# One transfer of 128 rows per tile for the last stores of an attention and SwiGLU kernel, in place of two of 64 rows

## The chip, the cores and the metric

The kernel runs on one core of a Trainium2 chip. The metric is the device time of one execution in microseconds (us); the figure quoted for a kernel is the median of its runs. One further execution is taken with the hardware profiler. Its "span" runs from the first to the last instruction on the core, and its own device time is a little longer than that span.

## The reference

```python
def _attn_ref(q, k, v):                       # each (8, 8, 576, 64), float32
    ...
    def phi(x, c, s):
        r = np.maximum(x, 0.0)
        return np.concatenate([r * c, r * s], axis=-1)
    q_p = phi(q, cos_w, sin_w)
    k_p = phi(k, cos_w, sin_w)
    kv = np.einsum('bhsf,bhsd->bhfd', k_p, v)
    z = np.sum(k_p, axis=2)
    num = np.einsum('bhsf,bhfd->bhsd', q_p, kv)
    den = np.einsum('bhsf,bhf->bhs', q_p, z)[..., None] + 1e-06
    return (num / den).astype(np.float32)

def _moe_ref(x, w_gate, w_val, w_out):        # x (4608, 512); weights 512x1536, 512x1536, 1536x512
    g = x @ w_gate
    silu = g * (1.0 / (1.0 + np.exp(-g)))
    val = x @ w_val
    return (silu * val @ w_out).astype(np.float32)

def reference(**kwargs):
    attn_out = _attn_ref(...)
    x = np.ascontiguousarray(attn_out.transpose(0, 2, 1, 3)).reshape(B * S, H * D)
    return _moe_ref(x=x, ...)
```

The output is 4608 rows of 512 float32 values, 9.44 MB.

## The kernel before

The linear attention of the eight batches is computed first for each batch, and its 4608 rows then go through the gated feed-forward block in nine groups (`tg` 0 to 8) of 512 rows. In each group the gate and value projections (line 990) are followed by the output product (line 1155); from group 1 on these products are done on 2x2 blocks, with seven block products in place of eight, so that sums of blocks stand beside them (`P1` to `P7` in `out_jobs`). Attention of later batches runs beside the feed-forward work of earlier groups.

Nothing is scheduled at run time. Every piece of work is a `Job` with a function, an engine and the jobs after which it comes; a table of job numbers, `ORDER`, says in which order the jobs are written into the program. Each engine then runs its own instructions in that order. The planner's figures in a `Job` (engine costs, `tail`, `dma`) aren't used when the table is there, except for the names of the engines.

An output tile is 128 rows of a group; a group has four (`t0` to `t0 + 3`). Rows of one batch are numbered so that a partition holds every ninth row:

```python
    out_v = out.rearrange("(b p c) f -> b c p f", p=SH, c=NC)      # SH = 64, NC = 9
```

So `out_v[b, c]` is 64 rows of the output that lie 9 x 512 values apart, and a tile of 128 partitions is two such sets: partitions 0 to 63 hold `c`, partitions 64 to 127 hold `c + 1`. The address in memory goes from row to row of one set by 4608 values, and from one set to the next by 512.

The results wait in SBUF in `ob` (groups 0 to 7) or, for the last group, in a part of `r_q` (`ob_last`), and are stored from there:

- `store_jobs` (line 1118) stores a tile of 512 columns by two transfers of 64 rows. In group 7, the second-last, tiles `t0` and `t0 + 1` go through the queue of SyncE (SP) and tiles `t0 + 2` and `t0 + 3` through that of GpSimd (POOL). The groups before use POOL alone, but for the first.
- In the last group each result quarter (256 columns of two tiles) is stored as it gets ready. `store_two_jobs` (line 1248) stores 64 rows of two tiles in one transfer, `store_tile_jobs` (line 1257) stores 64 rows of one tile. Of each pair one goes through SP's queue and the other through that of ScalarE (ACT).

The quarters of the last group get ready in this order: `e11` (tiles `t0`, `t0 + 1`, columns 0 to 255, one ACT operation, line 632), `e22` (tiles `t0 + 2`, `t0 + 3`, columns 256 to 511, two DVE operations, line 1212), `e21` (the same tiles, columns 0 to 255, two DVE operations, line 636) and `e12` (tiles `t0`, `t0 + 1`, columns 256 to 511, two DVE operations, line 636).

Transfers that SP and ACT issue signal their end through eight semaphores (`DMAHW0` to `DMAHW7`) that are taken in turn. A transfer waits, before it is issued, until the one eight places before it on these two queues has landed.

Of the kernel before, what the change touches and what calls it, by code (L numbers as in the profile page):

```python
# [18 lines left out]
def kernel(  # L19
# [10 lines left out]
    nc = tc.nc  # L30
# [4 lines left out]
    SH = 64  # L35
    NC = S // SH
    d_model, d_ff = moe_w_gate.shape
# [7 lines left out]
    NTG = NH // GH  # L45
# [4 lines left out]
    HD = d_model // 2  # L50
# [132 lines left out]
    def idle_products(n, cols=P):  # L183
# [34 lines left out]
        out=tab.rearrange("p c e d -> p (c e) d"),  # L218
        in_=csk.rearrange("p c e -> p (c e)").to_broadcast([P, NC * 2, D]),
# [31 lines left out]
    for j in range(2):  # L251
        t = (phi_all.rearrange("p a b -> p (a b)")[:, 0:V2_1].rearrange(
            "p (g c e w) -> p g c e w", g=G, c=NC, e=2) if j else
            consts.tile([P, G, NC, 2, W], BF16, name=f"v2_{j}"))
# [259 lines left out]
    for word in words:  # L514
        word, _, eng = word.partition("@")
        op, a, b = re.match(r"([A-Za-z]+)(\d+)\.?(\d*)", word).groups()
# [95 lines left out]
    def copies(n):  # L612
        return {"ACT": sc(n)}
# [24 lines left out]
    def relu_on(eng, out, in_):  # L638
        relu_op("act" if eng == "ACT" else "dve", out, in_)
# [25 lines left out]
    out_v = out.rearrange("(b p c) f -> b c p f", p=SH, c=NC)  # L665
# [450 lines left out]
        return res  # L1116

    def store_jobs(t, after, put, queues, cols=slice(0, d_model)):
        for e in range(2):
            q_ = queues[e]  # L1120

            def fn(j, e=e):
                idx = 2 * t + e
                {"POOL": nc.gpsimd, "SP": nc.sync, "ACT": nc.scalar}[j.eng].dma_start(  # L1124
                    out=out_v[idx // NC, idx % NC][:, cols], in_=ob_of(t)[e * SH:(e + 1) * SH, cols])
            Job({q_: 535 if q_ == "POOL" else 610}, fn, after=after, put=put, tail=1500.0, dma=(1450.0, 480.0))

    obs = {}

    def ob_of(t):  # L1130
        return pair_of(t // 2)[:, t % 2]

    def pair_of(p):
        return (ob_last if obs[p].kind == "last ob" else ob_all)[:, obs[p].at[0]]

    def out_jobs(tg, key):
        last = tg == NTG - 1
        t0 = tg * OUT
        ts = token_sum_jobs(tg)
        rooms = {n: Room("last ob" if last else "ob") for n in range(2)}  # L1140
# [6 lines left out]
        def product(n, rs, a, b, first, after, get=(), parts=((range(HC), (0, 1)),), keys=()):  # L1147

            res = []
            for m, (kcs, its) in enumerate(parts):  # L1150
                def fn(j, kcs=kcs, its=its):
                    for kc in kcs:
                        for i in its:
                            to = ps(rs[0])[:, i] if len(rs) == 1 else bank(rs[i])[:, 0:HD]
                            nc.tensor.matmul(out=to, lhsT=a[:, kc, i * P:(i + 1) * P], rhs=b[:, kc],  # L1155
                                             start=first and kc == 0 and i == 0, stop=kc == HC - 1, skip_group_check=True)
                at = keys[m] if m < len(keys) else (key[0], key[1] + (n + m / 4) * key[2])
                res.append(pe(len(kcs) * len(its) * 109.15, fn, at, after=after(kcs, its), behind=res, get=get if not m else ()))
            return res
# [3 lines left out]
        a, e = Room("bank", fills=True), Room("bank", fills=True)  # L1163
# [3 lines left out]
        def blk(w, jh):  # L1167
            return lambda kcs, its: blocks_of(tg, w, jh, sorted({kc // 2 for kc in kcs}))

        def summed(n, *more):  # L1170
            return lambda kcs, its: [ts[n][h] for h in sorted({kc // 4 for kc in kcs})] + tsum + sum(more, [])
# [31 lines left out]
            copied(j.eng, C(0, 0), ps(a), DOWN)  # L1203
        e11 = Job(copies(512), fn, after=P2, get=[rooms[0]], put=[a])
        if last:
            store_two_jobs(t0, slice(0, HD), [e11], ("SP", "ACT"))
        P5 = product(4, bs, S1, T1, False, lambda kcs, its: summed(1)(kcs, its) + ([ads[its[0]]] if last else ads), (), two)
        e22 = []
        for n, b_ in enumerate(bs):
# [2 lines left out]
                nc.vector.scalar_tensor_tensor(out=x, in0=p_, scalar=DOWN, in1=x, op0=ALU.mult, op1=ALU.add)  # L1212
            e22.append(Job({"DVE": d1(256 if last else 512)}, fn, after=P5[n:n + 1], behind=e22[-1:]))
        if last:
            store_two_jobs(t0 + 2, slice(HD, d_model), e22, ("SP", "ACT"))
        P4 = product(5, cs, aq[:, 1, 1], T4, False, lambda kcs, its: ([ads[its[0]]] if last else ads) + tsum + blk(1, 1)(kcs, its), (), two)
        e21 = []
        for n, c in enumerate(cs):
# [2 lines left out]
            e21.append(Job({"DVE": d1(256)} if last else copies(512), fn, after=P4[n:n + 1], put=[c]))  # L1221
        if last:
            for n in range(2):
                store_tile_jobs(t0 + 2, n, slice(0, HD), [e21[n]])
        else:
            for t in (t0 + 2, t0 + 3):
                store_jobs(t, e22 + e21, [rooms[1]], ("POOL", "POOL"))
        P3 = product(6, bs, S4, bq[:, 1, 1], False, lambda kcs, its: ts[4] + ([e22[its[0]]] if last else e22), (), two,
                     () if last or tg not in P3_AT else [(tg + 1, P3_AT[tg])])
        e12 = []  # L1230
# [4 lines left out]
            e12.append(Job({"DVE": d1(256)} if last else copies(512), fn, after=P3[n:n + 1], put=[b_]))  # L1235
        if last:
            for n in range(2):
                store_tile_jobs(t0, n, slice(HD, d_model), [e12[n]])
        else:
            for t in (t0, t0 + 1):  # L1240
                store_jobs(t, [e11] + e12, [rooms[0]], ("SP", "SP") if tg == NTG - 2 else ("POOL", "POOL"))
        J_["products", tg] = dict(P1=P1, P2=P2, P3=P3, P4=P4, P5=P5, P6=P6, P7=P7)
        J_["ht_free", tg, 0, 0] = P1 + ts[3] + ts[2]
        J_["ht_free", tg, 0, 1] = P5 + ts[2]
        J_["ht_free", tg, 1, 0] = P2 + ts[4]
        J_["ht_free", tg, 1, 1] = P4 + ts[1]

    def store_two_jobs(t, cols, after, queues):
        for e in range(2):
            def fn(j, e=e):  # L1250
                (b, c), (b1, _) = divmod(2 * t + e, NC), divmod(2 * t + 2 + e, NC)
                assert b == b1
                {"SP": nc.sync, "ACT": nc.scalar}[j.eng].dma_start(
                    out=out_v[b, c:c + 3:2, :, cols].rearrange("c p f -> p c f"),
                    in_=pair_of(t // 2)[e * SH:(e + 1) * SH, :, cols])
            Job({queues[e]: 660}, fn, after=after, tail=1300.0, dma=(700.0, 560.0))

    def store_tile_jobs(t, i, cols, after, queues=("SP", "ACT")):
        for e in range(2):
            def fn(j, e=e):  # L1260
                b, c = divmod(2 * (t + i) + e, NC)
                {"SP": nc.sync, "ACT": nc.scalar}[j.eng].dma_start(
                    out=out_v[b, c][:, cols], in_=pair_of(t // 2)[e * SH:(e + 1) * SH, i, cols])
            Job({queues[e]: 620}, fn, after=after, tail=1300.0, dma=(700.0, 280.0))

    def plain_out_jobs(key):
        rooms = [Room("ob"), Room("ob")]
# [33 lines left out]
    for lo, hi in ((0, 2), (2, 4)):  # L1301
        def fn(j, lo=lo, hi=hi):
            o = raws[1, "k"][:, lo:hi]
            relu_on(j.eng, o, o)
# [118 lines left out]
    for tg in range(1, NTG):  # L1423
        b = tg + 2
# [20 lines left out]
        for u in range(3):  # L1445
# [9 lines left out]
            rooms, silus = silu_jobs(tg, u, block_jobs(tg, u, "G", gate_order(tg, u)))  # L1455
# [3 lines left out]
            else:  # L1459
                for n, (i, w) in enumerate(((0, 0), (0, 1), (1, 0), (1, 1))):  # L1460
                    plain_val(tg, u, i, w, rooms, silus, at[f"v{n}"])
        out_jobs(tg, (tg, 3.05, 0.9 / 7))


# [69 lines left out]
    """  # L1534

    todo = set(jobs)
    for word in ORDER.split():
        n, e, at = re.match(r"(\d+)([av]?):?([\d,]*)", word).groups()
        j, at = jobs[int(n)], [int(x) for x in (at.split(",") if "," in at else at)]
# [36 lines left out]
```

## Time and profile before

| what | value |
|---|---|
| time, median of 3 runs | 299.13 us (298.21 to 299.59) |
| the profiled execution's own time | 298.66 us |
| its span | 296.8 us (so 1.86 us lie outside it) |
| TensorE (PE) busy | 290.1 us, 98% of the span |
| VectorE (DVE) / ScalarE (ACT) / GpSimd (POOL) busy | 252.9 / 199.1 / 69.1 us |
| mean granted TensorE clock | 0.996 |
| the last copy into the output buffer (DVE, line 636) | starts at 291.89 us, takes 0.42 us |
| stores of SP and ACT in the profile's end part | 10 on SP, 6 on ACT |

A profile line of instructions gives start, duration, engine, line of the kernel, operation and tiles written and read. "SPq" and "ACTq" are the issuing of transfers by these engines. The DMA rows give, for a stretch of time, the busy share of the 16 DMA engines and the rate in 40 equal slices (a digit is a tenth), then packets, MB and the time of these packets as a share of 16 engines for each queue. Queue q1 is SP's, q10 is ACT's and q0 POOL's. One packet here is one row of a store; small packets of 4 bytes come on top of them.

### The profile page before, as it was taken

Reading aid. Unit: us, or ns where it says so; the run is one execution under the profiler, and the core shown is the slowest. Engines: PE = TensorE matmul, PEld = TensorE weight load, DVE = VectorE, ACT = ScalarE, POOL = GpSimd, SP = SyncE. Lnnn points to the kernel's source line nnn. Section 1 sums busy time; section 2 is a strip of 40 time slices with the busy share of each in tenths; the row PEclk is TensorE's granted clock in tenths of the full one; section 3 lists DMA queues with packets and bytes.
Section 4 is the critical chain, followed back from the end, with each engine's and each line's share of the span. In section 5 each row is a group of like instructions: output and inputs, shape, how many; then the busy total and the mean of one; then the engine's idle time right before and its main releaser. Section 6 shows DMA issues by size and latency. Waiting matters only on the chain.

```text
span 296.8 us, 8157 instructions
## 1 busy us (share of the span) xinstructions
PE 290.1 (98%) x3292; PEld 237.7 (80%) x3292; DVE 252.9 (85%) x513; ACT 199.1 (67%) x423; POOL 69.1 (23%) x122
## 2 busy tenths in 40 slices
PE   8999999999999999999999999999999999999993
PEld 4697455665877888988898898888988898888882
DVE  7976889889987899999898977998778968968882
ACT  6664347978479868985499689976566555564630
POOL 7963530012015012213343020400050032002000
PEclk9999999999999999999999999999999999999998
DMA  7999999999969999599959947980270036000226
GB/s 255 232 196 198 202 206 209 229 202 155 170 149 171 199 209 144 102 172 148 209 118 159 197 68 131 208 146 2 38 171 8 2 89 127 0 2 18 55 53 161
DMA packets 71973, 40.90 MB, mean 138 GB/s; under 512 B 48768, under 2 KB 68736, under 8 KB 71936
## 3 DMA queue, kind: packets, MB, share of 16 engines
q0 software_dynamic: 24800, 24.39, 49.9%
q1 hardware_dynamic: 46528, 15.47, 27.6%
q10 hardware_dynamic: 608, 0.52, 0.6%
q8 instruction: 26, 0.43, 0.6%
q14 instruction: 11, 0.09, 0.1%
HBM read 37.75 MB, written 9.44 MB: 159 GB/s over the span
## 4 chain that ended last, share of the span: by engine, by line
PE 87%; DMA 9%; DVE 2%; issue 0%; DVEq 0%
PE banks L990 43%; PE banks L1155 23%; DMA xT<-x 4%; DMA phit<-r_q 4%; PE banks L440 4%; PE banks L917 4%; PE banks L1275 3%; PE banks L789 3%; PE banks L718 2%; PE banks L1065 2%; DMA wo_sb<-in_v_dram 1%; DVE v L292 1%; PE banks L371 1%; PE banks L784 1%; PE banks L1323 0%; PE banks L314 0%
## 5 line engine op out<-in xcount | busy, mean ns | idle before, releaser
L1124 POOL DMA_DIRECT2D out_dram<-ob x52 | 27.3, 532 | 128.4 <-ACT ob L632 87.6
L630 ACT COPY banks<-banks 128x512 f32<-128x512 f32 (+1 forms) x53 | 30.4, 577 | 22.3 <-PE banks L990 9.9
L1049 ACT ACTIVATE sg<-banks 128x512 bf16<-128x512 f32 x72 | 40.9, 599 | 5.8 <-PE banks L990 5.6
L1085 DVE TENSOR_TENSOR ht<-sg,banks 128x512 f16<-128x512 bf16 x60 | 40.4, 682 | 4.8 <-PE banks L990 4.4
L1155 PEld LDWEIGHTS <-ht 128*128 128x128 f16 x384 | 37.5, 98 | 4.5
L990 PEld LDWEIGHTS <-wg_sb 128*128 128x128 f16 x384 | 36.7, 98 | 5.3
L990 PEld LDWEIGHTS <-wgs_sb 128*128 128x128 f16 x368 | 35.4, 98 | 6.4 <-issue 0.5
L1010 DVE TENSOR_TENSOR banks<-m,banks 128x512 f32<-128x512 f32 x44 | 30.2, 692 | 7.3 <-PE banks L990 6.0
L990 PEld LDWEIGHTS <-wv_sb 128*128 128x128 f16 x320 | 31.2, 98 | 3.7
L990 PE MATMUL banks<-kvt,wgs_sb 128*128 128x256 f16 x236 | 33.8, 273 | 0.3 <-DVE kvt L963 0.3
L1155 PEld LDWEIGHTS <-sums 128*128 128x128 f16 x288 | 28.0, 98 | 3.4
L630 ACT COPY m<-banks 128x512 f32<-128x512 f32 x44 | 25.5, 590 | 5.7 <-PE banks L990 5.7
L990 PE MATMUL banks<-xT,wg_sb 128*128 128x256 f16 x192 | 28.6, 273 | 0.0
L632 ACT ACTIVATE ob<-banks 128x512 f32<-128x512 f32 x32 | 19.1, 596 | 10.6 <-PE banks L1155 9.3
L1155 PE MATMUL banks<-wo_sb,ht 128*128 128x256 f16 x192 | 25.2, 273 | 0.0
L990 PE MATMUL banks<-kvt,wg_sb 128*128 128x256 f16 x168 | 24.4, 273 | 0.0
L1155 PE MATMUL banks<-wt_sb,sums 128*128 128x256 f16 x192 | 24.2, 273 | 0.0
L820 DVE TENSOR_TENSOR x<-banks,rec 128x512 f16<-128x512 f32 x31 | 21.3, 690 | 3.1 <-PE banks L990 0.5
L990 PE MATMUL banks<-xT,wv_sb 128*128 128x256 f16 x160 | 23.8, 273 | 0.0
L1155 PE MATMUL banks<-wt_sb,ht 128*128 128x256 f16 x192 | 22.8, 272 | 0.0
L890 ACT ACTIVATE r_q<-raw_q,tanq 128x256 bf16<-128x256 bf16 x45 | 20.1, 507 | 0.0
L292 DVE TENSOR_TENSOR v<-raw_kv,tab 128x1152 bf16<-128x1152 bf16 x27 | 19.9, 750 | 0.0
(160 smaller groups left out, 540.1 us busy)
## 6 DMA issues: line engine op xcount, KB each, us to landing
out_dram<-ob POOLq DMA_DIRECT2D x52, 128.0 KB, 3.3
raw_kv<-in_k_dram POOLq DMA_DIRECT2D x7, 576.0 KB, 6.2
raw_q<-in_q_dram POOLq DMA_DIRECT2D x12, 288.0 KB, 9.9
raw_kv<-in_v_dram POOLq DMA_DIRECT2D x6, 576.0 KB, 9.3
out_dram<-ob SPq DMA_DIRECT2D x12, 128.0 KB, 2.8
wg_sb<-in_moe_w_gate_dram POOLq DMA_DIRECT2D x5, 256.0 KB, 9.0
wv_sb<-in_moe_w_val_dram POOLq DMA_DIRECT2D x5, 256.0 KB, 9.6
wo_sb<-in_v_dram SPq DMA_DIRECT2D x2, 576.0 KB, 4.1
```

Source lines behind the costliest of these rows:

```text
L292: nc.vector.tensor_tensor(out=v2s[b == 1][:, g, :, :, 0:D], in0=(first if b == 0 and g == 0 else {"v": raw_of(b, "v")})["v"][:, g].unsquee ...
L440: nc.tensor.matmul(out=st["f", tg, fc, lo][i], lhsT=(wg_sb, wv_sb)[i][:, kc, fs], rhs=xT[tg][:, ts, kc], start=(kc == 0), stop=(kc == KC - 1))
L630: nc.scalar.copy(out=out, in_=in_)
L632: nc.scalar.mul(out=out, in_=in_, mul=mul)
L820: tt(out=x_.rearrange("p (i y d) -> p i y d" if pairs else "p (y e d) -> p e y d", d=D, **({"i": 2} if pairs else {"e": 2})), in0=view()[: ...
L890: nc.scalar.activation(out=home()[:, :, c, 1], in_=raws[b, "q"][:, :, c], func=AF.Relu, scale=tanq[:, c:c + 1])
L990: nc.tensor.matmul(out=to[:, i], lhsT=a[:, c, 2 * u + i], rhs=x()[:, :, c], start=first and i == 0 and c == 0, stop=c == KH - 1, skip_grou ...
L1010: tt(out=bank(c), in0=one(m7_all, m).rearrange("p i x -> p (i x)"), in1=bank(b), op=ALU.add)
L1049: nc.scalar.activation(out=gates(rooms[w])[:, :, jh * HT:(jh + 1) * HT], in_=src, func=AF.Silu, scale=DOWN)
L1085: tt(out=ht[:, 4 * u + w:4 * u + w + 3:2, jh * HT:(jh + 1) * HT], in0=gates(rooms[w])[:, :, jh * HT:(jh + 1) * HT], in1=src.rearrange("p ( ...
L1124: {"POOL": nc.gpsimd, "SP": nc.sync, "ACT": nc.scalar}[j.eng].dma_start(out=out_v[idx // NC, idx % NC][:, cols], in_=ob_of(t)[e * SH:(e + ...
L1155: nc.tensor.matmul(out=to, lhsT=a[:, kc, i * P:(i + 1) * P], rhs=b[:, kc], start=first and kc == 0 and i == 0, stop=kc == HC - 1, skip_gro ...
```

## The change

Every store of the last group now carries one tile of 128 rows and 256 columns, and SP's stores of the second-last group carry one tile of 128 rows and 512 columns. The memory side of such a transfer is `out_v[b, c:c + 2]`, a view of 2 x 64 rows; the SBUF side is 128 partitions. POOL's stores and those of group 0 stay as they are. In `e22`'s stores, each waits for its own tile instead of for both.

```diff
     def store_jobs(t, after, put, queues, cols=slice(0, d_model)):
+        if len(queues) == 1 and 2 * t % NC < NC - 1:
+            return whole_tile_job(t, cols, after, queues[0], put, 6500.0)
         for e in range(2):
-            q_ = queues[e]
+            q_ = queues[e % len(queues)]
...
+    def whole_tile_job(t, cols, after, queue, put=(), tail=1300.0):
+
+        def fn(j):
+            b, c = divmod(2 * t, NC)
+            {"POOL": nc.gpsimd, "SP": nc.sync, "ACT": nc.scalar}[j.eng].dma_start(
+                out=out_v[b, c:c + 2][:, :, cols], in_=ob_of(t)[:, cols])
+        Job({queue: 600}, fn, after=after, put=list(put), tail=tail, dma=(700.0, 560.0))
...
         if last:
-            store_two_jobs(t0, slice(0, HD), [e11], ("SP", "ACT"))
+            for n in range(2):
+                whole_tile_job(t0 + n, slice(0, HD), [e11], ("SP", "ACT")[n])
...
         if last:
-            store_two_jobs(t0 + 2, slice(HD, d_model), e22, ("SP", "ACT"))
+            for n in range(2):
+                whole_tile_job(t0 + 2 + n, slice(HD, d_model), e22[n:n + 1], ("SP", "ACT")[n])
...
             for n in range(2):
-                store_tile_jobs(t0 + 2, n, slice(0, HD), [e21[n]])
+                whole_tile_job(t0 + 2 + n, slice(0, HD), [e21[n]], ("SP", "ACT")[n])
...
             for n in range(2):
-                store_tile_jobs(t0, n, slice(HD, d_model), [e12[n]])
+                whole_tile_job(t0 + n, slice(HD, d_model), [e12[n]], ("SP", "ACT")[n])
...
-                store_jobs(t, [e11] + e12, [rooms[0]], ("SP", "SP") if tg == NTG - 2 else ("POOL", "POOL"))
+                store_jobs(t, [e11] + e12, [rooms[0]], ("SP",) if tg == NTG - 2 else ("POOL", "POOL"))
...
-        1418:6 1406 1411 1412 1413 1409 1420 1426 1422 1423 1427 1308 1421:1 1428:0 1310 1309 1312 1429 1311 1410 1414
+        1416:6 1404 1409 1410 1411 1407 1418 1424 1420 1421 1425 1308 1310 1309 1419:1 1426:0 1428 1427 1408 1412
```

The rest of `ORDER` is the same jobs under numbers that are lower by two. On TensorE, VectorE and GpSimd the instructions and their order are the same as before.

On SyncE's queue the program ended with these stores (the size is that of the memory side, `ob` and `r_q` are the SBUF tiles, and the brackets name what is waited for):

```order
L1124 DMA out_dram<-ob 64x512 [waits DMAHW0_49,Activation_49]
L1124 DMA out_dram<-ob 64x512 [waits DMAHW1_49]
L1124 DMA out_dram<-ob 64x512 [waits DMAHW2_49]
L1253 DMA out_dram<-r_q 64x2x256 [waits DMAHW4_49,Activation_49]
L1124 DMA out_dram<-ob 64x512 [waits DMAHW5_49]
L1253 DMA out_dram<-r_q 64x2x256 [waits DMAHW7_49,DVE_49]
L1262 DMA out_dram<-r_q 64x256 [waits DMAHW1_49,DVE_49]
L1262 DMA out_dram<-r_q 64x256 [waits DMAHW3_49,DVE_49]
L1262 DMA out_dram<-r_q 64x256 [waits DMAHW5_49,DVE_49]
L1262 DMA out_dram<-r_q 64x256 [waits DMAHW7_49,DVE_49]
```

Ten transfers stand there, and each has 64 as the first of its memory side's dimensions. At the same place, from the last transpose on, SyncE now has these:

```order
L749 DMA_TRANSPOSE xT<-x 128x4x128 [waits DMAHW7_49,DVE_49]
L1134 DMA out_dram<-ob 2x64x512 [waits DMAHW0_49,Activation_49]
L1134 DMA out_dram<-ob 2x64x512 [waits DMAHW1_49]
L1134 DMA out_dram<-r_q 2x64x256 [waits DMAHW3_49,Activation_49]
L1134 DMA out_dram<-r_q 2x64x256 [waits DMAHW4_49,DVE_49]
L1134 DMA out_dram<-r_q 2x64x256 [waits DMAHW6_49,DVE_49]
L1134 DMA out_dram<-r_q 2x64x256 [waits DMAHW0_49,DVE_49]
```

Six transfers take the place of ten, the two of `ob` stand next to each other ahead of those of `r_q`, the first dimension on the memory side is 2, and the last one waits on the semaphore of the first store of `ob`.

On ScalarE's queue the six stores before were these:

```order
L1253 DMA out_dram<-r_q 64x2x256 [waits DMAHW3_49,Activation_49]
L1253 DMA out_dram<-r_q 64x2x256 [waits DMAHW6_49,DVE_49]
L1262 DMA out_dram<-r_q 64x256 [waits DMAHW0_49,DVE_49]
L1262 DMA out_dram<-r_q 64x256 [waits DMAHW2_49,DVE_49]
L1262 DMA out_dram<-r_q 64x256 [waits DMAHW4_49,DVE_49]
L1262 DMA out_dram<-r_q 64x256 [waits DMAHW6_49,DVE_49]
```

They come behind the last ACT operation, that of `e11`. From that operation on, ScalarE now has these:

```order
L632 ACTIVATE r_q<-banks 128x2x256 [waits PE_49]
L1134 DMA out_dram<-r_q 2x64x256 [waits DMAHW2_49,Activation_49]
L1134 DMA out_dram<-r_q 2x64x256 [waits DMAHW5_49,DVE_49]
L1134 DMA out_dram<-r_q 2x64x256 [waits DMAHW7_49,DVE_49]
L1134 DMA out_dram<-r_q 2x64x256 [waits DMAHW1_49,DVE_49]
```

Four transfers take the place of six, and the last of them waits on the semaphore of SP's second store of `ob`.

More of the change, by code (lines that the diff above doesn't have):

```diff
@@ L1125, in fn @@
                     out=out_v[idx // NC, idx % NC][:, cols], in_=ob_of(t)[e * SH:(e + 1) * SH, cols])
-            Job({q_: 535 if q_ == "POOL" else 610}, fn, after=after, put=put, tail=1500.0, dma=(1450.0, 480.0))
+            Job({q_: 560}, fn, after=after, put=put, tail=6500.0, dma=(1270.0, 480.0))
+    def whole_tile_job(t, cols, after, queue, put=(), tail=1300.0):
[4 more added lines that the diff above has]
+        Job({queue: 600}, fn, after=after, put=list(put), tail=tail, dma=(700.0, 560.0))
     obs = {}
@@ L1246, in out_jobs @@
         J_["ht_free", tg, 1, 1] = P4 + ts[1]
[L1248 to L1264, printed above, removed]
     def plain_out_jobs(key):
```

21 rows, old and new, of the table ORDER are left out of this document.

## The prediction

> **What bounds the kernel now.** I read the page first, for the engine that limits the span, then the chain of waits, and then the end of the trace: the queues of SyncE (SP) and ScalarE (ACT), and the DMA view in short stretches.
>
> ```profile
> span 296.8 us, 8157 instructions
> PE 290.1 (98%) x3292; PEld 237.7 (80%) x3292; DVE 252.9 (85%) x513; ACT 199.1 (67%) x423; POOL 69.1 (23%) x122
> ...
> 282.68 9.18 PE banks L1155 x84
> 291.87 0.02 issue
> 291.89 0.42 DVE r_q L636
> ```
>
> TensorE is busy for 98% of the span and the chain runs through it to 291.87 us. One DVE copy follows and ends at 291.89 + 0.42 = 292.31. The change leaves all instructions of TensorE, VectorE and GpSimd in place, so nothing before the first changed store, at 285.20, can move. What the change can touch is what lies behind 292.31: 296.8 - 292.31 = 4.5 us in which only stores are issued, moved and waited for. The SP and ACT queues there, from the timeline:
>
> ```profile
> 285.20 1.76 SPq L1124 DMA_DIRECT2D out_dram<-ob  x3
> 288.58 0.65 SPq L1253 DMA_DIRECT2D out_dram<-r_q  x1
> 289.28 0.61 SPq L1124 DMA_DIRECT2D out_dram<-ob  x1
> 289.99 1.16 SPq L1253 DMA_DIRECT2D out_dram<-r_q  x1
> ...
> 288.59 2.56 ACTq L1253 DMA_DIRECT2D out_dram<-r_q  x2
> 291.25 2.82 ACTq L1262 DMA_DIRECT2D out_dram<-r_q  x4
> ...
> 293.86 0.55 SPq L1262 DMA_DIRECT2D out_dram<-r_q  x1
> ```
>
> The last store is issued at 293.86, 1.55 us behind the copy that it stores. SP still had three other stores of line 1262 to issue and doesn't get to it earlier. So the number of issues does cost something at the end, and halving it is worth up to 1.5 us. The next view is the DMA one for 288.5 to 296.8 us:
>
> ```profile
> DMA  0000301897999511899999847499799791000000
> GB/s 0 0 0 0 79 0 44 197 168 153 306 365 390 183 40 39 212 188 178 267 341 326 296 158 212 124 222 227 173 207 237 168 222 45 0 0 0 0 0 0
> DMA packets 1297, 1.20 MB, mean 144 GB/s; under 512 B 208, under 2 KB 1232, under 8 KB 1296
> q1 hardware_dynamic: 688, 0.66, 32.0%
> q10 hardware_dynamic: 608, 0.52, 21.4%
> ...
> out_dram<-r_q SPq DMA_DIRECT2D x2, 128.0 KB, 3.3
> out_dram<-r_q ACTq DMA_DIRECT2D x2, 128.0 KB, 3.9
> out_dram<-r_q SPq DMA_DIRECT2D x4, 64.0 KB, 2.0
> out_dram<-r_q ACTq DMA_DIRECT2D x4, 64.0 KB, 2.0
> ```
>
> A slice is 8.3 / 40 = 0.2075 us. The last slice with data is the 34th, so data end at 288.5 + 34 x 0.2075 = 295.55, and the span ends 1.25 us after that. In the best slice, the 13th, the engines are at "9" and move 390 GB/s, 24.4 GB/s for each of the 16. The row of q10 tells how a store is divided: ACT issued 2 transfers of 128 KB and 4 of 64 KB, in rows of 1 KB that is 2 x 128 + 4 x 64 = 512 packets, and q10 counts 608. The other 96 are small ones, 16 for each of the 6 transfers. Thus each store of 64 rows was divided over all 16 engines, and each engine closed its share with a small packet.
>
> **The change, part by part.** *What is kept.* The same 1.57 MB go out in ten transfers in place of sixteen: two of `ob` with 128 rows of 2 KB (0.524 MB) and eight of `r_q` with 128 rows of 1 KB (1.049 MB). The dependencies are as before, except that `e22`'s first store waits for one DVE operation less (0.42 us in the row of such an operation above). This makes it earlier and can cost nothing.
>
> *What is saved.* SP issues 6 stores instead of 10, ACT 4 instead of 6. This is the 1.55 us above, if transfers still take as long as they did.
>
> *What is new: the memory side of each transfer.* Its first dimension was 64 and is now 2 (2 x 64 rows; a tile's two halves lie 512 values apart, its rows 4608). No row of the trace shows a transfer whose first dimension is below 64, so the division of such a transfer has to be bounded from both sides: 16 shares, as every store of the trace has, or 2 shares, one for each step of the first dimension. I take 2. In the stores of before, a share is a run of whole steps of the first dimension (64 / 16 = 4 of them) at one distance. The new 128 rows have no single distance, and 2 steps can't make 16 runs. On this point the Trainium skill, in "DMA: Bandwidth & Descriptors", section "Rules for kernel authors", says that the number of engines follows from the slowest dimension of the two access patterns that isn't 1, and that an outermost dimension of size c below 16 holds the whole transfer to at most c engines. By that rule the sum is the one below. The packet row agrees with it where the first dimension is 64 (16 shares), and no run here shows it for 2.
>
> *The price of two shares.* If all ten transfers run on the same two engines, each engine carries 1.573 / 2 = 0.786 MB. The fast end is the best slice, 24.4 GB/s for one engine: 32.2 us. The slow end is the mean of packet times. In the view above the two queues spent (0.320 + 0.214) x 16 x 8.3 = 70.9 us of engine time on 1.18 MB, 60 us for a MB. The stores of `ob` were slower still; the DMA view of 286.2 to 288.4 us has them alone:
>
> ```profile
> DMA packets 240, 0.39 MB, mean 179 GB/s; under 512 B 48, under 2 KB 48, under 8 KB 240
> q1 hardware_dynamic: 240, 0.39, 78.1%
> ```
>
> That is 0.781 x 16 x 2.2 = 27.5 us for 0.39 MB, 70.5 us for a MB. By these, one engine needs 0.262 x 70.5 + 0.524 x 60 = 18.5 + 31.5 = 50 us. The slow rows come from 16 engines that write at once, 144 to 179 GB/s together. Two engines ask for no more than 2 x 24.4 = 49 GB/s together, so they are nearest to the fast row. I take 33 us, and keep 32 and 50.
>
> *When it starts and whether the two engines ever run dry.* The first data packet of these stores is in the DMA view of 284 to 286.5 us, in slices of 0.0625 us:
>
> ```profile
> DMA  0000000000000000000000000000000000000947
> GB/s 0 0 0 0 0 0 0 0 0 0 0 0 0 0 0 0 0 0 0 0 0 0 0 0 0 0 0 0 0 0 0 0 0 0 0 0 0 229 131 197
> ```
>
> It starts at 284 + 37 x 0.0625 = 286.3, 1.1 us behind the issue at 285.20, and stays there, since the first store of `ob` still waits for the same ACT copy. The two `ob` stores alone are 0.262 MB for each engine, 10.7 us at the fast price, to 297.0. By then the last copy (292.31) is long done. Two waits are new at the end: SP's last store waits for the first `ob` store to land and ACT's last for the second. If the two queues take turns packet by packet, the second `ob` store has landed at about 302. ACT's other three stores put 192 packets on each engine, and only some 90 of them are through at that time. The engines therefore still have work, and the waits cost nothing; nothing is queued behind these two stores but the end of the program.
>
> *The sum*, against the profiled execution's 298.66 us: data from 286.3, 33 us on the two engines, to 319.3; 1.25 us to the end of the span, 320.55; 298.66 - 296.8 = 1.86 us outside it, 322.4. The saved issues don't count here, since the engines have a backlog all the time. The median of before, 299.13, stands 0.47 above the profiled execution, so on that scale it is 322.9 us, 23.8 us or 8% slower.
>
> **The rivals.** *Sixteen shares after all* (not slower). If the rows are divided over all engines as before, SP's and ACT's last stores are issued right behind the last copy, at 292.33 instead of 293.86. Each share has 8 rows instead of 4, which adds 4 KB at 24.4 GB/s, 0.17 us. The gain is 1.53 - 0.17 = 1.4 us at most, 297.3 against 298.66 or 297.7 on the median's scale. It is smaller if ACT needs 1.28 us for each issue of 128 rows, as the row of its two stores of line 1253 has it (2.56 / 2): four of them from 288.59 on end at 293.71, only 0.7 us before today's last issue ends (293.86 + 0.55). For it speak the 16 small packets for each transfer, against it the argument of the distance. The Trainium skill, same page and section, also has a rule that points to this rival: it says that two transfers to separate halves of the partitions gain nothing over one of 128 partitions, and to use the one. The trace shows only the two halves. The point from which this rival decides: with n engines the data end at 286.3 + 64.4 / n, and this comes before today's 295.55 from n = 7 on.
>
> *Two engines at the slow price.* If a 1 KB or 2 KB packet takes as long with two engines as with 16, the 50 us count: 286.3 + 50 + 1.25 + 1.86 = 339.4, or 339.9 on the median's scale. For it speaks that the `ob` stores took the slow price with no other queue beside them; against it that 390 GB/s were reached a few us later.
>
> *A pair of engines for each queue.* If SP's transfers go to one pair and ACT's to another, SP's pair has the most, 0.262 + 0.262 = 0.524 MB for each engine, 21.5 us: 286.3 + 21.5 + 1.25 + 1.86 = 310.9. No row speaks for it: both queues used all 16 engines.
>
> **How the numbers follow.** Forecast (the same two engines, near the fast price) 0.74; sixteen shares 0.12; slow price 0.10; separate pairs 0.04. The predicted time is that of the forecast, 322.9. Its own range is 318 to 330, for a share somewhat faster than the best slice or partly slowed. For 8 in 10 the slow price has to be in, so the range is 318 to 340; sixteen shares and separate pairs (0.16) stay out. A measurement of this kernel can tell about 0.5%, 1.5 us, from no change. Of the 0.12 for sixteen shares, a gain of 1.4 us or less stays mostly within that: 0.08 for the same, 0.04 for faster. All else is slower, 0.88.
>
> **What would show it.** TensorE's end and the last DVE copy stay at about 291.9 and 292.3 us. If the forecast holds, the DMA share from 286.5 on is at 2 of 16 engines, about 0.12, at some 49 GB/s, up to about 319. ACT's queue then has 512 + 4 x 2 = 520 packets instead of 608, and the last stores take over 15 us to land where rows of before show 2.0. If q10 has 512 + 4 x 16 = 576 packets and the span ends near 295.5, the first rival is right. Two engines with a share above 33 us, or 0.12 kept up to 336, mean the slow price, and a share of 0.25 the separate pairs. The prediction is wrong altogether if the queue ends before 310 us.

## The result and the profile after

The changed kernel takes 323.26 us (median of 4 runs, 322.85 to 324.03) against 299.04 us (4 runs) for the kernel before. The ratio is 1.0816 with a 95% interval of 1.0782 to 1.0849: 8% slower, where 322.9 us was forecast. The profiled execution took 323.02 us.

The page of the changed kernel, its head and the rows of its 40 slices (8.0 us each):

```profile
span 321.0 us, 8147 instructions
PE 290.4 (90%) x3292; PEld 238.1 (74%) x3292; DVE 252.7 (79%) x513; ACT 199.0 (62%) x423; POOL 68.3 (21%) x122
PE   8999999999999999999999999999999999993000
DMA  7999999989799988998995896026008000201111
GB/s 270 215 200 198 201 207 217 233 151 174 152 165 211 191 129 105 190 164 160 142 189 83 148 197 131 2 46 155 0 8 184 10 2 0 67 11 52 49 48 38
```

TensorE is as busy as before (290.4 and 290.1 us). It now stands idle in the last three slices, in which the DMA engines are at "1", a tenth, and move 49, 48 and, in the slice in which the data end, 38 GB/s. The end of the chain of waits, and the issues of the two queues behind 284 us:

```profile
282.25 9.19 PE banks L1165 x84
291.43 0.02 issue
291.46 0.42 DVE r_q L636
...
284.77 1.19 SPq L1134 DMA_DIRECT2D out_dram<-ob  x2
288.15 20.29 SPq L1134 DMA_DIRECT2D out_dram<-r_q  x4
...
288.15 14.61 ACTq L1134 DMA_DIRECT2D out_dram<-r_q  x4
```

The computation ends at 291.46 + 0.42 = 291.88 us, as before (292.31; the place of this copy moved between 291.9 and 293.8 over the profiles of this study, and what follows is therefore counted from the copy). All that was added lies behind it: 321.0 - 291.88 = 29.1 us, where it was 4.5. The DMA view of 284 to 321 us (slices of 0.925 us):

```profile
DMA  0011111111111111111111111111111111111100
GB/s 0 0 18 35 31 62 49 49 51 49 52 48 52 51 50 50 50 49 49 49 49 48 48 49 49 49 48 48 49 49 48 48 49 49 49 48 48 49 9 0
DMA packets 1301, 1.59 MB, mean 43 GB/s; under 512 B 20, under 2 KB 1044, under 8 KB 1300
q1 hardware_dynamic: 780, 1.05, 8.1%
q10 hardware_dynamic: 520, 0.52, 4.0%
```

The same bytes as before go out, at 49 GB/s in place of up to 390. "Under 512 B" counts the small packets with which each engine closes its share of a transfer: 20 for ten transfers, 2 each. ACT's queue has 520 packets, 512 rows and 4 x 2 small ones.

### The profile page after: what moved, and what is told of

Same layout as the page of the kernel before. It is cut to its first block, busy times and chain, and to the rows that moved or that the text cites. A ratio compares the mean times of both kernels' runs of the same rounds, so it can differ in the third digit from the quotient of the medians.

```text
span 321.0 us, 8147 instructions
## 1 busy us (share of the span) xinstructions
PE 290.4 (90%) x3292; PEld 238.1 (74%) x3292; DVE 252.7 (79%) x513; ACT 199.0 (62%) x423; POOL 68.3 (21%) x122
## 4 chain that ended last, share of the span: by engine, by line
PE 90%; ACT 0%; DVE 0%; issue 0%
PE banks L990 42%; PE banks L1165 23%; PE banks L1065 4%; PE banks L1269 3%; PE banks L440 3%; PE banks L917 3%; PE banks L186 3%; PE banks L718 3%; PE banks L789 2%; PE banks L371 1%; PE banks L784 1%; PE banks L1317 0%; PE banks L314 0%; PE banks L420 0%; PE banks L350 0%; PE banks L757 0%
## 5 line engine op out<-in xcount | busy, mean ns | idle before, releaser
L1165 PE MATMUL banks<-wo_sb,ht 128*128 128x256 f16 x192 | 25.2, 273 | 0.0
L990 PE MATMUL banks<-kvt,wg_sb 128*128 128x256 f16 x168 | 24.4, 273 | 0.0
L1165 PE MATMUL banks<-wt_sb,sums 128*128 128x256 f16 x192 | 24.2, 273 | 0.0
```

Source lines behind the costliest of these rows:

```text
L990: nc.tensor.matmul(out=to[:, i], lhsT=a[:, c, 2 * u + i], rhs=x()[:, :, c], start=first and i == 0 and c == 0, stop=c == KH - 1, skip_grou ...
```

## The experiments

The theory was that the first dimension of a transfer's memory side sets the number of engines, and that the time is the bytes of each engine at 24.4 GB/s. Rival A: a transfer of 128 rows in one issue is slow in itself. Rival B: memory that is written at the two distances of 512 and 4608 values is slow, with any number of engines.

### One distance for all 128 rows

```diff
-                out=out_v[b, c:c + 2][:, :, cols], in_=ob_of(t)[:, cols])
+                out=out[6 * S:].rearrange("(p c) f -> c p f", c=NC)[{28: 2, 29: 3, 32: 4, 33: 5, 34: 6, 35: 1}[t]][:, cols],
+                in_=ob_of(t)[:, cols])
```

> The changed kernel with the same ten transfers, in the same order, of the same 128 rows and bytes; only the memory side is another: 128 rows at one distance of 4608 values (first dimension 128 instead of 2), which puts the rows of the last two groups in other places of the output, so its output isn't the reference's. Theory (the number of engines follows the first dimension on the memory side): 16 engines again, 297.5 us, between 297 and 299.5, and ACT's queue with 576 packets instead of 520. Rival A (a transfer of 128 rows in one issue is slow in itself): about 323 us. Rival B (what is slow is memory written at two short distances, 512 and 4608 values, whatever the number of engines): 297.5 us as well, but with 520 packets.

Measured: 298.05 us (9 runs), ratio 0.9960 (0.9943 to 0.9977). Its DMA view of 284 to 297.4 us (slices of 0.335 us):

```profile
GB/s 0 0 0 0 0 0 0 0 0 0 190 367 385 385 239 0 0 0 0 0 196 324 318 306 318 58 9 18 193 348 337 346 330 55 24 0 0 0 0 0
DMA packets 1441, 1.59 MB, mean 119 GB/s; under 512 B 160, under 2 KB 1184, under 8 KB 1440
q10 hardware_dynamic: 576, 0.52, 11.7%
```

160 small packets for ten transfers are 16 each, and q10 has the 576 packets of the theory. Ten transfers of 128 rows, issued in the same order with the same bytes, are no slower than the sixteen of before. Rival A falls. Against rival B speaks the number of packets, but the distances changed with the number of engines here; the next two runs keep them.

### First dimension 4 and 8

```diff
-                out=out_v[b, c:c + 2][:, :, cols], in_=ob_of(t)[:, cols])
+                out=out_v[b, [2, 1][t >= 32] + 4 * (t >= 34):][0:4, 32 * (t % 2):32 * (t % 2) + 32, cols], in_=ob_of(t)[:, cols])
```

> The changed kernel with each of its ten transfers written as 4 x 32 rows on the memory side (distances 512 and 4608 values as before), which again puts rows in other places. Theory: 4 engines, half of the changed kernel's 33.4 us of data: 16.7 us from about 286, to 302.6, span near 304, time 305 to 306.5 us. Rival A and rival B: 323 us, since neither the size of a transfer nor the distances change.

```diff
-                out=out_v[b, c:c + 2][:, :, cols], in_=ob_of(t)[:, cols])
+                out=out_v[b, 1:9, 16 * (t % 4):16 * (t % 4) + 16, cols], in_=ob_of(t)[:, cols])
```

> As the run with 4 x 32 rows, but 8 x 16 rows. Theory: 8 engines need 8.3 us for all the data, which would end at about 294.5 if all of it were ready at 286; the last copy is ready at 292.3, so the end is set by the last stores as in the kernel before: 297.5 to 300 us. Rivals A and B: 323 us.

Measured: 308.66 us (2 runs), ratio 1.0316 (1.0281 to 1.0350), with 4; 300.26 us (10 runs), ratio 1.0042 (1.0024 to 1.0060), with 8. From 284 us to the end, the DMA view of the run with 4 (slices of 0.57 us), then that of the run with 8 (0.3525 us):

```profile
DMA  0000032122322222222222222222222222221000
GB/s 0 0 0 0 11 32 11 25 65 83 129 97 101 101 97 92 99 83 88 97 97 95 97 95 97 97 95 97 95 97 97 95 97 95 97 92 43 0 0 0
DMA packets 1321, 1.59 MB, mean 70 GB/s; under 512 B 40, under 2 KB 1064, under 8 KB 1320
```

```profile
DMA  0000000005533555554755555555555555510000
GB/s 0 0 0 0 0 0 0 0 17 81 41 41 128 180 198 198 192 209 186 215 186 174 192 166 192 189 189 166 198 177 192 189 198 189 183 47 0 0 0 0
DMA packets 1361, 1.59 MB, mean 113 GB/s; under 512 B 80, under 2 KB 1104, under 8 KB 1360
```

Small packets for each of the ten transfers: 4 and 8. The busy share is at 2 tenths (4 of 16) and 5 tenths (8 of 16). The rate is 97 and about 190 GB/s, which with the 49 of two engines is 24 GB/s for an engine each time. Rival B falls too, since the distances are the same in all three. Both times are longer than the theory had them, by 2.2 to 3.7 us with 4, and by 0.3 us beyond the upper end with 8. The first slices with data show most of it: 11 to 65 GB/s with 4 engines for some 2.9 us before the later rate is reached, which costs about 2 us at 97 GB/s. This slow start wasn't in the theory and is taken up below. With 8 engines the theory also had the data through before the last stores; the rate stays at about 190 GB/s up to the end of the data, so 8 engines still had a backlog there.

### As many transfers, with 64 first

```diff
+    def pair_job(t, e, cols, after, queue, put=()):
+        def fn(j):
+            b, c = divmod(2 * t + e, NC)
+            {"SP": nc.sync, "ACT": nc.scalar}[j.eng].dma_start(
+                out=out_v[b, c:c + 3:2, :, cols].rearrange("c p f -> p c f"),
+                in_=pair_of(t // 2)[e * SH:(e + 1) * SH, :, cols])
+        Job({queue: 660}, fn, after=after, put=list(put))
...
-                whole_tile_job(t0 + n, slice(HD, d_model), [e12[n]], ("SP", "ACT")[n])
+                pair_job(t0, n, slice(HD, d_model), e12, ("SP", "ACT")[n])
```

> As many transfers as in the changed kernel (6 on SP, 4 on ACT) with as many bytes in each, and the reference's output: each transfer carries one half (64 partitions) of two tiles, as 64 x 2 rows, so that the first dimension is 64 on both sides. Each waits for both of its tiles' copies. Theory: 16 engines; SP's last issue starts behind the last copy (292.33 instead of 293.86), so up to 1.4 us under the kernel before: 297.3 to 299 us. Rival A: 323 us. Rival B: 297.3 to 299 us. If the saved issues are worth nothing, 299 us.

Measured: 299.19 us (12 runs), ratio 0.9997 (0.9981 to 1.0012). So the number of transfers and the bytes in each aren't what costs 8%. The hoped-for gain isn't there either. The end of its chain of waits, its last two issues (from the timelines of both queues at 293.5 to 294.5 us), the queues in its DMA view from 284 us on, and the landing of these last two stores (DMA view of 293.6 to 295 us):

```profile
293.21 0.43 DVE r_q L636
...
293.67 0.60 SPq L1142 DMA_DIRECT2D out_dram<-r_q  x1
293.67 0.64 ACTq L1142 DMA_DIRECT2D out_dram<-r_q  x1
...
q1 hardware_dynamic: 864, 1.05, 32.4%
q10 hardware_dynamic: 576, 0.52, 11.1%
...
out_dram<-r_q SPq DMA_DIRECT2D x1, 128.0 KB, 2.5
out_dram<-r_q ACTq DMA_DIRECT2D x1, 128.0 KB, 2.8
```

The copy ends at 293.64 and both queues issue at 293.67, 0.03 us later where it was 1.55 us. But the last stores now carry 128 KB instead of 64, and take 2.5 and 2.8 us to land where those of 64 KB took 2.0. From the copy to the end of the span are 297.8 - 293.64 = 4.2 us, where it was 4.5. Of the 1.5 us by which the last issue is earlier, the longer last transfer takes back 0.5 to 0.8. Only 0.3 us are left in this profile, and nothing in the median of the runs; where the rest goes, behind the landing, is open.

### Each part alone

The last group alone (SP's stores of the second-last group as before):

```diff
-                store_jobs(t, [e11] + e12, [rooms[0]], ("SP",) if tg == NTG - 2 else ("POOL", "POOL"))
+                store_jobs(t, [e11] + e12, [rooms[0]], ("SP", "SP") if tg == NTG - 2 else ("POOL", "POOL"))
```

> The part of the change in the last group alone: its eight stores as in the changed kernel (2 x 64 rows), SP's stores of the second-last group as before (four of 64 rows). Theory: the stores of ob go over 16 engines and are through early; the eight stores put 0.524 MB on each of two engines, 512 packets at the 42 ns at which they follow each other in the changed kernel, 21.7 us from about 289.7 on: data to 311.4, time 314.5 us (312 to 316). A rival by which the ob transfers in front of the queue cost the time (they hold up SP): 300 us. A rival by which only the last stores matter: 323 us.

SP's stores of the second-last group alone, in the kernel before (with `store_jobs` and `whole_tile_job` as in the changed kernel):

```diff
-                store_jobs(t, [e11] + e12, [rooms[0]], ("SP", "SP") if tg == NTG - 2 else ("POOL", "POOL"))
+                store_jobs(t, [e11] + e12, [rooms[0]], ("SP",) if tg == NTG - 2 else ("POOL", "POOL"))
```

> The other part alone: SP's two stores of ob as in the changed kernel (2 x 64 rows of 2 KB), the twelve stores of the last group as before. Theory: two engines carry 128 packets of 2 KB for ob (10.2 us and a slow start of 1 to 2 us) and besides their sixteenth of all other stores, 64 packets of 1 KB (2.7 us): they end at about 301 instead of 295.5, so 304 us; as the second ob store lands late and SP's tenth transfer waits for it, with two more queued behind it on SP, up to 308 us. So 303 to 308. If ob stores are hidden by the work that follows them: 299 us.

Measured: 316.98 us (2 runs), ratio 1.0603 (1.0573 to 1.0633), for the last group alone; 306.3 us (2 runs), ratio 1.0246 (1.0213 to 1.0278), for the two `ob` stores alone. The DMA view of the first from 284 us on (0.7725 us) and, for the second, its SP queue, the longest wait there and its DMA view (0.5275 us):

```profile
GB/s 0 0 0 148 186 210 135 27 27 29 27 28 33 49 48 48 48 49 49 48 48 48 49 49 48 48 48 49 49 48 48 48 50 48 48 48 48 49 3 0
```

```profile
288.99 3.05 SPq L1263 DMA_DIRECT2D out_dram<-r_q  x2
292.13 10.49 SPq L1272 DMA_DIRECT2D out_dram<-r_q  x4
...
SPq L1272 <- DMA out_dram<-ob: 8.0, 1, 8.0
...
GB/s 0 0 0 0 0 23 16 31 23 31 43 85 70 165 247 210 208 153 177 216 107 150 50 56 62 99 134 80 50 47 50 31 23 4 124 118 95 35 0 0
```

Both parts cost, each for itself. With the last group alone the four `ob` stores pass at up to 210 GB/s, and then two engines are left: 27 to 33 GB/s for six slices and 48 to 50 after that. The time is 2.5 us above the theory's 314.5 and outside the range, again by the slow start. With the two `ob` stores alone the wait that the expectation named is there: a store of line 1272 waits 8.0 us until the second `ob` store has landed, and two more are queued behind it. The two costs are 17.9 and 7.3 us and add up to 25.2, near the 24.2 us of both together. The sum alone doesn't show two shares of one backlog: with the last group alone the backlog lasts up to the end of the data, while with the two `ob` stores alone the 8.0 us wait sets the end, and the last data come in separate bursts behind it.

### GpSimd for the stores that stand in SP's way

```diff
-                store_jobs(t, [e11] + e12, [rooms[0]], ("SP", "SP") if tg == NTG - 2 else ("POOL", "POOL"))
+                store_jobs(t, [e11] + e12, [rooms[0]], ("POOL", "POOL"))
```

> The kernel before with SP's four stores of the second-last group issued by GpSimd, whose queue is empty there; all else as before, 64 rows each. SP then has eight stores in place of twelve behind 285 us, and the transfer that its second store of line 1262 waits for is another one. If issuing (and that wait) sets the last 1.55 us, SP's last store is issued at about 292.9 instead of 293.86: 1 us less, 298.1 us. If not, 299.1 us. If GpSimd's transfers land late or get in the way, slower.

Measured: 298.54 us (12 runs), ratio 0.9989 (0.9976 to 1.0001). This goes the expected way, at half the size or less, and the interval just includes no change. The last copy of this run and SP's last store (timeline of 294 to 296 us):

```profile
292.10 0.42 DVE r_q L636
...
293.74 0.57 SPq L1262 DMA_DIRECT2D out_dram<-r_q  x1
```

The last store comes 1.22 us behind the end of its copy (292.52), where it was 1.55 us; it was expected at 0.6. Four issues less on SP's queue are thus worth 0.3 us of the 1.55, since the four issues of line 1262 still follow each other. In the second run of this kind GpSimd takes `e22`'s two stores as well:

```diff
-            store_two_jobs(t0 + 2, slice(HD, d_model), e22, ("SP", "ACT"))
+            store_two_jobs(t0 + 2, slice(HD, d_model), e22, ("POOL", "POOL"))
```

> The kernel before with the four ob stores and the two stores of e22 issued by GpSimd, 64 rows on the memory side's first dimension everywhere. SP and ACT then have five stores each. If the queueing of issues behind the last copy is what is left at the end, SP's and ACT's last stores are issued at about 292.4 instead of 293.86 and 293.58: 1.4 us less, 297.7 us. If a store of 64 rows by itself needs the time from the last copy on (issue 0.55, landing 2.0, end 0.9), no more than about 1 us is to be had: 298.1 us. If GpSimd's stores of e22 land late (3.3 us in the profile before), they still land by 293.5 and cost nothing.

Measured: 301.34 us (6 runs), ratio 1.0067 (1.0048 to 1.0086), slower, where 297.7 to 298.1 us was expected. The last two stores on its GpSimd queue, the last of its chain of waits, what SP waited for from 284 us on, the DMA view of 294 to 299.4 us (slices of 0.135 us), and the rows of GpSimd's DRAIN instructions at the end of the program, of this run and then of the run with 298.54 us:

```profile
290.74 1.22 POOL L1253 DMA_DIRECT2D out_dram<-r_q  x2 [2.70 <-issue]
...
292.38 0.42 DVE r_q L636
...
SPq L1571 <- PEq L1571: 2.9, 2, 2.4
SPq L1571 <- DMA out_dram<-r_q: 2.3, 1, 2.3
...
DMA  7899997421000000000000000000000000000000
...
L1571 POOLq DRAIN  x3: 51/102/7383, 291.2 to 299.1; - x3
...
L1571 POOLq DRAIN  x3: 51/102/7212, 287.0 to 296.6; - x3
```

Data end at 294 + 10 x 0.135 = 295.35, 2.55 us behind the copy's end (292.80). In the kernel before it was 3.2 us (295.5 and 292.31), so the shorter queues gave 0.6 us. But the span ends at 299.4, 4.0 us after the data, where it was 1.3. The extra time is in the program's last instructions (line 1571, waits of 2.9 us on SP that aren't for stores). A row of DRAIN gives the number, the shortest, median and longest duration in ns, and the first and last start. The longest stands behind GpSimd's last store: it starts at 291.2 and takes 7.38 us, so GpSimd goes on only at 298.6, long after the data. The wait view names TensorE's queue for SP's longest wait, 2.4 us, but GpSimd is the one that isn't through. In the version with 298.54 us the same DRAIN takes 7.21 us from 287.0 on and is over at 294.2, before the data end. Every run has it, with 7.2 to 7.8 us; only here does it last into the end of the program. Why it takes so long is open.

## Why the prediction was right, point by point

- *Nothing ahead of the stores moves.* TensorE's busy time is 290.4 us instead of 290.1, and the last copy ends at 291.88.
- *Two shares for each transfer.* Shown by the 20 small packets, and by the runs with 4, 8 and 128 as first dimension, which have 4, 8 and 16 for each transfer at 24 GB/s an engine up to 8. The rule of the Trainium skill that the prediction weighed ("DMA: Bandwidth & Descriptors", "Rules for kernel authors": an outermost dimension below 16 limits the engines) agrees in every one of them. The other rule of that section of the Trainium skill, to use one transfer of 128 partitions in place of two halves, agrees by 0.4% with the run with one distance (ratio 0.9960), and not with the changed kernel.
- *The price, 33 us.* Data run from 285.9 (the first slice with data in the view of 285 to 289 us below) to 319.3: 33.4 us. The choice of the fast row was right. The size was right partly by luck, since the steady rate alone gives 32.2 us and the rest is the slow start, which no step had in it:

```profile
DMA  0000000001104003011130011500011210112011
GB/s 0 0 0 0 0 0 0 0 0 41 41 0 41 0 0 41 0 41 41 41 41 0 0 41 61 61 0 0 0 41 61 41 20 0 41 41 82 20 41 61
DMA packets 46, 0.09 MB, mean 24 GB/s; under 512 B 0, under 2 KB 0, under 8 KB 46
```

- *The end.* Data stop in the 13th of 40 slices of 318.5 to 321 us, at 318.5 + 13 x 0.0625 = 319.3; the span ends 1.7 us later, where 1.25 was taken. The end of the data is the forecast's 319.3 because a start 0.4 us earlier and a stretch of data 0.4 us longer than taken cancel. The 0.45 us more behind the data and 2.0 us outside the span instead of 1.86 make up the 0.6 us between the 322.4 worked out for the profiled execution and its 323.02.

```profile
GB/s 33 66 33 66 33 66 33 66 33 49 49 49 49 0 0 0 0 0 0 0 0 0 0 0 0 0 0 0 0 0 0 0 0 0 0 0 0 0 0 0
q1 hardware_dynamic: 40, 0.04, 4.4%
```

- *The engines never run dry, and the new waits cost nothing.* From 294 us on the rate stands at 48 to 52 GB/s up to the end. ACT's last store was issued at 301.04 (row below), after a wait for the second `ob` store, which was forecast for about 302. The wait is read from the order of the program, which names it, and from the 4.0 us between this issue and the end of the one before (290.60 + 6.48 = 297.08).
- *The rivals.* Sixteen shares, the slow price and separate pairs are all excluded by the one view: 2 small packets for each transfer, 49 GB/s for both queues together. The first rival's gain, up to 1.4 us, can be read from two runs. The run with one distance is its form, 128 rows over 16 engines, and was 1.0 us faster than the kernel before by the medians (0.4%); its issues took 0.35 us in the median, so the 1.28 us for an issue of 128 rows, which the prediction allowed for, didn't come. The run with pairs of 64, which writes the reference's rows, gained nothing: where the prediction counted 0.17 us for a share twice as long, the last store took 0.5 to 0.8 us longer to land.
- *What is saved was misread in one point.* The prediction puts the 1.55 us behind the last copy down to the number of issues. But between its four stores of line 1262 SP also waited 0.8 us for an earlier store of `r_q` to land (the row below, from SP's waits at 286 to 296.8 us in the kernel before), and with four issues fewer ahead of them the last store came only 0.3 us earlier. The saving had no part in the sum.

```profile
SPq L1262 <- DMA out_dram<-r_q: 0.8, 1, 0.8
```

- *The landing of the last stores.* The prediction wanted to see the last stores take over 15 us to land. The profile gives no such time for the transfers with fewer than 16 shares here, but SP's last store was issued at 303.21, and the last packets, which are all of its queue (q1 in the view of 318.5 to 321 us), end at 319.3: 16.1 us.

## What to carry to other kernels

Before two transfers are merged, look at the first dimension that the merged one has on each side: 2 x 64 rows is another transfer than 128 rows, and the small packets for each transfer, or the busy share of the 16 engines, tell at once how many engines work on it. For a store that ends a kernel, a first dimension of 64 or 128 rows gave all 16 engines here, and one of 2, 4 or 8 gave only as many. Fewer issues gain little where the last transfer gets longer for it. A queue of another engine isn't free of cost at the program's end either: look how long that engine's last instructions run on behind its stores.

## What the runs showed of the hardware that was not expected

*The issuing engine is held up as well.* An issue of line 1262 takes about 0.55 us in the kernel before (median; on line 1253 up to 1.4). In the changed kernel single issues take up to 7.5 us, by the timelines of SP and of ACT cut into stretches:

```profile
288.15 1.81 SPq L1134 DMA_DIRECT2D out_dram<-r_q  x1
290.06 7.48 SPq L1134 DMA_DIRECT2D out_dram<-r_q  x1
303.21 5.22 SPq L1134 DMA_DIRECT2D out_dram<-r_q  x1
...
290.60 6.48 ACTq L1134 DMA_DIRECT2D out_dram<-r_q  x1
301.04 1.73 ACTq L1134 DMA_DIRECT2D out_dram<-r_q  x1
```

With 4 engines the longest took 2.7 us, with 8 engines 1.5, hardly more than in the kernel before. Only other stores were queued behind these issues. In the middle of a kernel, ACT's own work would presumably stand behind such an issue for 6.5 us; no run tried it.

*A slow start on few engines.* In each run whose transfers were on 2, 4 or 8 engines the first 1.8 to 4.6 us ran at a third to two thirds of the later rate (27 to 33 against 49 GB/s in the run with the last group alone, 11 to 65 against 97 with four). By these rates it cost 1 to 2 us each time. The two engines of the changed kernel weren't idle in it: in the view of 285 to 289 us above, 46 packets of 2 KB took 9.8% of 16 engines (row below), 6.3 us of engine time and 136 ns for each, where the later rate gives 84 ns. With 16 engines and one distance the first slice that is full already has 367 GB/s. What makes the packets take longer is open; no run was made for it.

*The time of SP's packets.* With one distance over 128 partitions SP's 864 packets took 22.4% of 16 engines in 13.4 us (row below), 48 us of engine time. With pairs of 64 partitions the same bytes took 32.4% of 13.8 us, 72 us. The number of partitions alone doesn't explain it: ACT's stores, also of 128 partitions in the one run and 64 in the other, took 11.7% and 11.1%, 25 us each time. The distances differ as well, so the cause is open. The run with one distance is the only one whose interval lies below the kernel before.

```profile
q1 hardware_dynamic: 46, 0.09, 9.8%
...
q1 hardware_dynamic: 864, 1.05, 22.4%
```
